# Attention before a mixture of experts: a shorter argmax chain, a first pair taken head by head, and batch 0's routing moved to the last pair

## The chip, the cores and the metric

The kernel runs on one core of one Trainium2 chip. The metric is the device time of one execution in microseconds (us). The engines are TensorE (PE; its weight loads, PEld, overlap its matmuls), VectorE (DVE), ScalarE (ACT), GpSimd (POOL) and SyncE (SP), which issues most DMAs. TensorE's clock has two levels, 1.2 and 2.4 GHz; a row's granted clock of 0.50 is the lower one.

## The reference

Only attention and the routing bear on the change. A query sees the keys of its own cluster; a token goes to one of eight experts.

```python
q_assign = np.argmax(np.einsum('bhsd,hcd->bhsc', q_n, c_n), axis=-1)
k_assign = np.argmax(np.einsum('bhsd,hcd->bhsc', k_n, c_n), axis=-1)
mask = q_assign[:, :, :, None] == k_assign[:, :, None, :]
scores = np.where(mask, scale * np.matmul(q, k.transpose(0, 1, 3, 2)), -1000000000.0)
attn = np.exp(scores - np.max(scores, axis=-1, keepdims=True))
out = np.matmul(attn / (np.sum(attn, axis=-1, keepdims=True) + 1e-09), v)
logits = x @ w_gate
e_idx = np.argmax(logits, axis=1)
```

Batch 2, heads 8, sequence 768, head size 64, 16 clusters. The expert layer (8 experts, 512 to 1024 to 512) and a dense layer (512 to 2048 to 512) follow.

## The kernel before

Attention takes two heads of a batch as a pair: pairs 0 to 3 are batch 0, pairs 4 to 7 batch 1. A head has six tiles of 128 queries, so a pair is 12 steps and attention 96. `run` (L476) goes through iterations i from -1. Iteration i issues the score matmuls of step i+1 (`qk_mm`, L363: two groups of QA by KA over 128 rows, two of QB by KB over 80, which hold the masks in rows 64 to 79), the softmax of step i (`soft`, L386: a reduction on VectorE, an exponential on ScalarE), the next stage of step i-1 and, seven steps late, the product with V (`pv`, L449). The last pair is cut in two groups of tiles so that routing can begin early.

Probabilities must be transposed. A third of the steps, and all of the last pair, do it on TensorE (`onpe`, L376; `turn`, `high`, `low2`). The others convert to 16 bits (`soft` on ScalarE, or `low` on VectorE where `dve`, L382, says so), GpSimd subtracts the low part (L438), and SP transposes two steps by DMA (L442), followed by one zero fill of a routing table from `bgdma`, if any is left.

Beside this runs the preparation of the next pair, placed by step in a list (`plan`, L256) that is written out by hand: load of q and k (L169), split in high and low halves (`halves`, L323), eight transposing tasks (`turned`, L172, with copies of half a head by DMA, L298), scores against the centroids (`scores`, L184), the argmax chain (`best`, L195), and the masks (`masks`, L333), which ScalarE evicts and four DMAs of SP put in place. The V of a pair's heads is scaled and split on GpSimd (`split_v`, L146); the scale of a batch is found by `load_v` (L114). A task at r runs in iteration base + r; within an iteration the first half of its tasks stand ahead of `pv`, the rest behind it.

Pair 0 has nothing ahead of it: `first` (L214) splits and transposes both heads, finds both argmaxes and then makes the masks (`masks1`, L344); `setup` (L65) normalises the centroids. Up to L501 the program's order is left to a scheduler; from there on each engine keeps the written order (L580).

When a pair's output is done, `pair` (L675) transposes it and adds its share of the router's logits; after a batch's last pair `route` (L709) picks experts, ranks the tokens (matmuls into `rk`), and scatters six tiles of rows by indirect DMA on GpSimd (`scatter`, L777). `run` takes one stage of it per iteration, and two where i - base is 9. Three PSUM buffers of the tag T serve all transposes, scores and routing; two hold scores of steps, one the output.

## Time and profile before

| | us |
|---|---|
| three runs | 834.8, 837.65, 840.44 |
| median of the runs | 837.65 |
| profiled execution | 835.05 |
| its span, first to last instruction | 833.1 |

The span is what the rows below count from. The clock line is TensorE's granted clock. Shares of busy time are averages over stages with different limits. The stages, by time: lead-in to 26.84, eight pairs to 292.67, the last outputs and routing to 324.77, experts to about 550, the dense layer to the end.

### The profile page before, as it was taken

To read this page: it belongs to the slowest core of one execution; us is meant where nothing else is said; L and a number is where in the kernel's file an instruction comes from. 1 tells how busy PE (TensorE), PEld (TensorE's weight loads), DVE (VectorE), ACT (ScalarE), POOL (GpSimd) and SP (SyncE) were. 2 spreads that over 40 slices of the span, in tenths; PEclk is the share of its full clock that TensorE was granted. 3 is DMA by queue.
4 is the path that set the end of the run, shared out by engine and by line. 5 is a ranking of instruction groups with operands and counts; after the bars stand their busy time and mean duration, and the time that the engine had idled before them with its cause. 6 is when DMAs were issued, how large, how long until landed. Compare 5 with 4: busy or idle time off the path is not lost. (4 is left out here: it accounts for less than half of the span.)

```text
span 833.1 us, 14096 instructions
## 1 busy us (share of the span) xinstructions
PE 760.7 (91%) x5478; PEld 642.5 (77%) x5478; DVE 486.5 (58%) x879; ACT 430.3 (52%) x695; POOL 326.4 (39%) x269
## 2 busy tenths in 40 slices
PE   5869889998899868999999999889999999999996
PEld 5658878987788755888897887667678788878885
DVE  5777797787758757466654677489932322231222
ACT  3666877867747534465555666477822322221221
POOL 1578677777775025645343455145510000000000
PEclk9979999889979977999999999999999999999999
DMA  5199999896696326688664874555500100010001
GB/s 155 23 213 245 206 205 197 174 180 148 159 165 103 123 103 225 219 291 271 221 217 150 299 233 142 190 212 173 181 1 1 51 0 1 1 50 1 1 0 54
DMA packets 132648, 116.31 MB, mean 140 GB/s; under 512 B 97719, under 2 KB 103863, under 8 KB 132576
## 3 DMA queue, kind: packets, MB, share of 16 engines
q1 hardware_dynamic: 128624, 106.27, 47.7%
q0 software_dynamic: 3952, 9.08, 3.8%
q8 instruction: 44, 0.72, 0.3%
q14 instruction: 28, 0.23, 0.1%
HBM read 71.67 MB, written 18.45 MB: 108 GB/s over the span
## 5 line engine op out<-in xcount | busy, mean ns | idle before, releaser
L859 POOL TENSOR_TENSOR w<-stage,w 128x512 fp32r<-128x512 f32 (+1 forms) x54 | 102.5, 1903 | 120.5 <-ACT w L854 109.5
L1190 PE MATMUL hp<-XH,w 128*128 128x512 f32 (+1 forms) x392 | 125.4, 397 | 2.5 <-DVE sg L1197 2.1
L854 ACT ACTIVATE w<-stage 128x1024 fp32r<-128x1024 f32 (+1 forms) x104 | 96.3, 940 | 51.4 <-DMA stage<-in_moe_w 25.2
L394 ACT ACTIVATE p<-sp,m 128x768 f32<-128x768 f32 x96 | 86.7, 903 | 54.0 <-DVE m L392 53.7
L1169 PE MATMUL op<-w,GH 128*128 128x512 f32 x384 | 112.2, 394 | 0.0
L392 DVE TENSOR_REDUCE m<-sp 128x1 f32<-128x768 f32 x96 | 91.4, 952 | 28.9 <-PE sp L373 28.4
L438 POOL TENSOR_TENSOR p<-p,p 128x768 f16<-128x768 f32 x58 | 95.3, 1650 | 30.6 <-DVE p L437 23.5
L1197 DVE TENSOR_TENSOR sg<-hp,sg 128x512 f32<-128x512 f32 (+1 forms) x49 | 33.3, 679 | 117.5 <-ACT sg L1196 117.4
L955 PEld LDWEIGHTS hp<-X,w 128*128 128x128 f32 x672 | 86.7, 191 | 9.8 <-DVE HL L958 5.5
L955 PE MATMUL hp<-X,w 128*128 128x256 f32 x672 | 90.8, 285 | 3.0 <-DVE HL L958 2.1
L1190 PEld LDWEIGHTS hp<-XH,w 128*128 128x128 f32 x392 | 74.0, 190 | 21.4 <-DVE sg L1197 3.5
L1196 ACT ACTIVATE sg<-hp 128x512 f32<-128x512 f32 (+1 forms) x49 | 28.9, 589 | 116.7 <-PE hp L1190 115.6
L859 DVE TENSOR_TENSOR w<-stage,w 128x1024 fp32r<-128x1024 f32 x50 | 69.0, 1386 | 31.3 <-ACT w L854 29.9
L1169 PEld LDWEIGHTS op<-w,GH 128*128 128x128 f32 x384 | 71.9, 188 | 17.1 <-ACT GH L854 0.4
L462 PE MATMUL o<-vh,pt 128*128 128x66 f16 x576 | 67.3, 202 | 11.7 <-DVE xb L471 6.7
L1190 PE MATMUL hp<-XL,w 128*128 128x512 f32 (+1 forms) x196 | 75.7, 394 | 1.9 <-DVE XL L859 1.9
L462 PEld LDWEIGHTS <-pt 128*128 128x128 f16 x576 | 55.7, 101 | 19.3 <-issue 11.9
L1169 PE MATMUL op<-w,GL 128*128 128x512 f32 x192 | 68.3, 397 | 1.7 <-DVE GL L859 1.7
L371 PE MATMUL sp<-KA,QA 128*128 128x384 f32 x192 | 64.9, 421 | 4.7 <-ACT p L394 4.4
L463 PE MATMUL o<-vl,pt 128*128 128x64 f16 x576 | 66.8, 198 | 0.0
L464 PE MATMUL o<-vh,pt 128*128 128x66 f16 x576 | 66.6, 199 | 0.2 <-DVE pt L429 0.2
L972 PE MATMUL yp<-w,HH 128*128 128x512 f32 x224 | 64.0, 400 | 1.5 <-ACT HH L957 1.5
(210 smaller groups left out, 1477.1 us busy)
## 6 DMA issues: line engine op xcount, KB each, us to landing
stage<-in_moe_w SPq DMA_DIRECT2D x72, 512.0 KB, 4.7
stage<-in_moe_w_in SPq DMA_DIRECT2D x16, 512.0 KB, 4.2
stage<-in_moe_w_out SPq DMA_DIRECT2D x16, 512.0 KB, 3.9
xst<-z SPq DMA_DIRECT2D x16, 258.0 KB, 3.3
xt<-xst SPq DMA_DIRECT2D x7, 516.0 KB, 4.2
vt<-in_v SPq DMA_DIRECT2D x4, 768.0 KB, 7.6
xt<-x SPq DMA_DIRECT2D x6, 512.0 KB, 4.7
out_x<-os SPq DMA_DIRECT2D x12, 256.0 KB, 2.3
```

What stands on the lines that cost most here:

```text
L371: nc.tensor.matmul(sp[:, g, :384], lhsT=QA[:, t], rhs=KAf[:, g * 384:(g + 1) * 384], start=True, stop=False)
L392: st['min'] = nc.vector.tensor_reduce(m, sv, axis=AX.XY, op=ALU.min).ins
L394: st['exp'] = nc.scalar.activation(p32, sv, AF.Exp, bias=m, scale=-1.0).ins
L438: s.nc.gpsimd.tensor_sub(p16[:, 1], p32, p16[:, 0])
L462: nc.tensor.matmul(o[:, t, 0:D + 2], lhsT=pt[:, 0, kt], rhs=vh[:, kt], start=kt == 0, stop=False)
L463: nc.tensor.matmul(o[:, t, 0:D], lhsT=pt[:, 0, kt], rhs=vl[:, kt], start=False, stop=False)
L464: nc.tensor.matmul(o[:, t, 0:D + 2], lhsT=pt[:, 1, kt], rhs=vh[:, kt], start=False, stop=kt == NT - 1)
L854: s.nc.scalar.activation(hi, src, AF.Copy)
L859: (eng or s.nc.vector).tensor_sub(lo, src, hi)
L955: nc.tensor.matmul(hp, lhsT=W1[k][w][:, f * 128:(f + 1) * 128], rhs=x[:, k, :N], start=n == 0, stop=n == 11)
L1169: nc.tensor.matmul(op[i], lhsT=g[:, i * 128:(i + 1) * 128], rhs=w, start=f == 0 and m == 0, stop=f == 15 and m == 2)
L1190: nc.tensor.matmul(h, lhsT=I[k, f // 8][w][:, fs], rhs=x[:, k, c], start=n == 0, stop=n == 11)
```

## The change

The argmax chain becomes six operations on one PSUM tile, with the high and low score side by side, and both masks come from one comparison; the query mask is turned round where it is evicted, by a factor and a bias. `first` takes head 0 to its masks before head 1's scores; head 1's subtractions and copies go to GpSimd, and its chain into the first steps. The written order holds from the first load. 12 matmuls on a constant run ahead of all. `plan` is made once, with absolute steps; a half (x.5) stands behind `pv`. V's diagonal products go to ScalarE; VectorE converts steps 8 and 9 of 12 instead of 4, 5 and 8. Zero fills begin with step 12. `high` stands ahead of the deferred evictions, and `low2` at the end of the tasks. Batch 0's `route` is kept back and taken up at iteration 86. Stages of the router per iteration follow two lists.

```diff
+    def warm(s, n):
+
+        o = s.ps_o.tile([128, NT, D + 2], F32, tag='o', name='warm')
+        for _ in range(n):
+            s.nc.tensor.matmul(o[:, 0:5].rearrange('p t d -> p (t d)')[:, 0:256], lhsT=s.ones, rhs=s.ones.unsqueeze(1).to_broadcast([128, 2, 128]), start=True, stop=True)
+
     def setup(s):
...
+                yield
         nc.vector.tensor_tensor(r, r, ss, op=ALU.mult)
...
+        nc.vector.tensor_sub(qv[:, :, 1], kv[:, :, 0], tv)
+        yield
 
     def consts(s):
...
-        nc.vector.tensor_scalar(s.mcol, mi, BIG / 16, 1.0, op0=ALU.mult, op1=ALU.max)
+        nc.vector.tensor_scalar(s.mcol, mi, (BIG + 1) / 16, -1.0, op0=ALU.mult, op1=ALU.add)
+        s.mbias = c.tile([64, 1], F32, name='mbias')
+        nc.vector.tensor_scalar(s.mbias, mi, -1.0 / 16, 1.0, op0=ALU.mult, op1=ALU.add)
...
-        nc.vector.tensor_scalar(dg[:, 1], s.ident[0:8, 0:8], g, None, op0=ALU.mult)
+        nc.scalar.activation(dg[:, 1], s.ident[0:8, 0:8], AF.Copy, scale=g)
...
-        nc.vector.tensor_scalar(dg[:, 0], s.ident[0:8, 0:8], rg, None, op0=ALU.mult)
+        nc.scalar.activation(dg[:, 0], s.ident[0:8, 0:8], AF.Copy, scale=rg)
...
-    def scores(s, hd):
+    def scores(s, hd, sides=(0, 1), clb=None):
...
-        s.clb = clb = s.T('cl')
-        cl = clb[:, :2 * NT * 2 * C].rearrange('p (a t w c) -> p a t w c', a=2, t=NT, w=2)
-        for a, (A, c1) in enumerate(((QA, s.cQ), (KA, s.cK))):
+        if clb is None:
+            clb = s.T('cl')
+        cl = clb[:, :2 * NT * 2 * C].rearrange('p (a t x) -> p a t x', a=2, t=NT)
+        for a in sides:
+            A, c1 = ((QA, s.cQ), (KA, s.cK))[a]
...
     def best(s, clb, oh, j):
 
...
-        for a in (1, 0):
-            nc.vector.tensor_reduce(s0[:, a], cl[:, a].rearrange('p t w c -> p t c w'), axis=AX.X, op=ALU.add)
-        yield
-        nc.vector.tensor_reduce(mx, s0, axis=AX.X, op=ALU.max)
-        nc.vector.tensor_tensor(s1, s0, mx.unsqueeze(3).to_broadcast([128, 2, NT, C]), op=ALU.is_ge)
-        yield
-        nc.vector.tensor_tensor(s1, s1, s.rev.unsqueeze(1).unsqueeze(1).to_broadcast([128, 2, NT, C]), op=ALU.mult)
-        nc.vector.tensor_reduce(mx, s1, axis=AX.X, op=ALU.max)
-        nc.vector.tensor_tensor(oh[:, :, j, 0], s1[:, 0], mx[:, 0].unsqueeze(2).to_broadcast([128, NT, C]), op=ALU.not_equal)
-        nc.vector.tensor_tensor(oh[:, :, j, 1], s1[:, 1], mx[:, 1].unsqueeze(2).to_broadcast([128, NT, C]), op=ALU.is_equal)
+        n = 2 * NT
+        mx = s.sm2.tile([128, n], F32, tag='mx', name='mx')
+        bc = mx.unsqueeze(2).to_broadcast([128, n, C])
+        x = clb[:, 0:n * C].rearrange('p (n c) -> p n c', c=C)
+        nc.vector.tensor_reduce(x, clb[:, 0:2 * n * C].rearrange('p (n c w) -> p n c w', w=2, c=C), axis=AX.X, op=ALU.add)
+        yield
+        nc.vector.tensor_reduce(mx, x, axis=AX.X, op=ALU.max)
+        nc.vector.tensor_tensor(x, x, bc, op=ALU.is_ge)
+        yield
+        nc.vector.tensor_tensor(x, x, s.rev.unsqueeze(1).to_broadcast([128, n, C]), op=ALU.mult)
+        nc.vector.tensor_reduce(mx, x, axis=AX.X, op=ALU.max)
+        yield
+        nc.vector.tensor_tensor(oh[:, :, j].rearrange('p t a c -> p a t c'), x.rearrange('p (a t) c -> p a t c', a=2), bc.rearrange('p (a t) c -> p a t c', a=2), op=ALU.is_equal)
         yield
 
...
+        hds = [s.heads(2 * hp + j, j) for j in range(2)]
+        lo = (nc.vector, nc.gpsimd)
+
+        def split(j):
             js = slice(j, j + 1)
             nc.scalar.activation(nq[:, js, :, 0], qt[:, js], AF.Copy)
-            nc.vector.tensor_sub(nq[:, js, :, 1], qt[:, js], nq[:, js, :, 0])
+            lo[j].tensor_sub(nq[:, js, :, 1], qt[:, js], nq[:, js, :, 0])
             nc.scalar.activation(nk[:, js, :, 1], kt[:, js], AF.Copy)
-            nc.vector.tensor_sub(nk[:, js, :, 0], kt[:, js], nk[:, js, :, 1])
-            hd = s.heads(2 * hp + j, j)
-            for n, A, w in ((nq, hd[1], -0.125), (nk, hd[3], 1.0)):
+            lo[j].tensor_sub(nk[:, js, :, 0], kt[:, js], nk[:, js, :, 1])
+
+        def turn(j):
+            for n, A, w in ((nq, hds[j][1], -0.125), (nk, hds[j][3], 1.0)):
                 for half in range(2):
                     s.turned(A, n, j, half, w)
                     s.flush()
-            nc.gpsimd.tensor_copy(hd[2][0:64], hd[1][0:64])
-            nc.vector.tensor_copy(hd[4][0:64], hd[3][64:128])
-            out.append(hd)
-            yield 'setup'
-        for j in range(2):
-            s.scores(out[j])
-            for _ in s.best(s.clb, oh, j):
-                pass
-        for j in range(2):
-            yield from s.masks1(oh, out[j], j)
-            s.ready[b, hp, j] = out[j]
-            yield 'head'
+        split(0)
+        turn(0)
+        yield
+        nc.gpsimd.tensor_copy(hds[0][4][0:64], hds[0][3][64:128])
+        split(1)
+        nc.scalar.activation(hds[0][2][0:64], hds[0][1][0:64], AF.Copy)
+        clb = s.scores(hds[0], (1, 0))
+        turn(1)
+        for _ in s.best(clb, oh, 0):
+            pass
+        nc.gpsimd.tensor_copy(hds[1][2][0:64], hds[1][1][0:64])
+        nc.gpsimd.tensor_copy(hds[1][4][0:64], hds[1][3][64:128])
+        for _ in s.masks1(oh, hds[0], 0):
+            pass
+        s.ready[b, hp, 0] = hds[0]
+        yield
+        clb = s.scores(hds[1])
+        yield
+        yield from s.best(clb, oh, 1)
+        yield from s.masks1(oh, hds[1], 1)
+        s.ready[b, hp, 1] = hds[1]
+        yield
 
     def out(s):
         if s.oev:
...
-        if pi + 2 < len(pairs):
-            add(3 if g0 else -1, lambda: s.load_qk(*pairs[pi + 2]))
...
-        if z:
-            for r in (-1, 0, 0, 1, 1):
-                add(r, nx(g0))
-            for r in (3, 3, 4, 4, 5, 6, 6, 6):
-                add(r, nx(vg))
-        for h, r in enumerate((7, 9) if z else (1, 2)):
-            add(r, sp(h))
-        if pi == 1:
-            s.v1 = s.load_v(1)
-        for r in {1: (3, 6, 10), 2: (6, 10), 3: (4, 5, 6, 6)}.get(pi, ()):
+        for r in (-0.5, 0.0, 0.5, 1, 1.5, 2, 2.0, 2.0):
+            add(r, nx(g0))
+        for r in (1.5, 1.5, 2, 3.5, 3.5, 4.5, 6, 7.0):
+            add(r, nx(vg))
+        s.v1 = s.load_v(1)
+        for r in (14.0, 17.5, 24.0, 32.0, 35.0, 40.0, 41.0, 42.0, 42.5):
             add(r, nx(s.v1))
-        if pi + 1 < len(pairs):
-            b, hp = pairs[pi + 1]
...
-            tr8 = [(j, a, half) for j in range(2) for a in range(2) for half in range(2)]
-            for (j, a, half), r in zip(tr8, (2, 2, 3, 3, 4, 4, 5, 5) if z else (-1, -1, -1, 0, 0, 0, 3, 3)):
-                add(r, lambda j=j, a=a, half=half: tr(j, a, half))
-            for j, (r, r1, r2, r3) in enumerate(((4, 5, 6, 7), (7, 8, 8, 9)) if z else ((1, 2, 3, 4), (4, 5, 6, 7))):
-                add(r, lambda j=j: sc(j))
-                for q in (r1, r2, r3):
-                    add(q, bst(j))
...
-            add(9 if z else 8, m)
-        if pi + 2 < len(pairs):
-            for i, r in enumerate((7, 8) if not z else (8, 10)):
-                add(r, lambda i=i: s.halves(pairs[pi + 2], i))
+        for p, (b, hp) in enumerate(pairs):
+            o = 12 * p
+            for h, r in enumerate((8.0, 8.5) if p == 0 else (0.0, 1.5)):
+                add(o + r, lambda b=b, h=2 * hp + h: s.split_v(b, h))
+            if p:
+                s.prepare(add, p, pairs[p], o - 12)
...
+        if not z:
+            add(1.5 if p == 2 else o - 12 + -2.0, lambda: s.load_qk(b, hp))
+        for i, r in enumerate((0.5, 1.0) if z else (6.5, 8.5) if p == 2 else [o - 12 + r for r in (6.0, 7.0)]):
+            add(r, lambda i=i: s.halves(pair, i))
...
+        tr8 = [(j, a, half) for j in range(2) for a in range(2) for half in range(2)]
+        for x, r in zip(tr8, (1.5, 1.5, 2.0, 2.5, 3.5, 3.5, 5.5, 5.5) if z else (-1.5, -0.5, 0.0, 0.5, 0.5, 0.5, 3.5, 3.5)):
+            add(o + r, lambda x=x: tr(*x))
+        for (j, a), r in zip(((0, 0), (0, 1), (1, 0), (1, 1)), (4.0, 5.0, 7.0, 7.0) if z else (1.0, 1.0, 4.0, 4.0)):
+            add(o + r, lambda j=j, a=a: sc(j, a))
+        for i, r in enumerate((7.0, 7.0, 7.0, 7.5, 8.5, 9.5, 9.5, 9.5) if z else (2.5, 2.5, 4.5, 4.5, 5, 5.0, 6.0, 7.5)):
+            add(o + r, lambda j=i // 4: next(ch[j]))
...
+        add(o + (9.5 if z else 8.0), m)
...
-        s.defer.append(lambda: nc.scalar.activation(mk, mp[0:64, :NT * 128].rearrange('p (t n) -> p t n', t=NT), AF.Copy, scale=s.mcol))
+        s.defer.append(lambda: nc.scalar.activation(mk, mp[0:64, :NT * 128].rearrange('p (t n) -> p t n', t=NT), AF.Identity, scale=s.mcol, bias=s.mbias))
...
-                    nc.scalar.activation(dst, src, AF.Copy)
+                    nc.scalar.activation(dst, src, AF.Copy, scale=-1.0, bias=1.0)
...
-        return st['i'] % 12 in (4, 5, 8)
+        return st['i'] % 12 in (8, 9)
...
-                if s.bgdma:
+                if s.bgdma and i >= 12:
...
+        traced = nc.cur_bb.bb.instructions
+        first = len(traced)
...
+        s.load_qk(*pairs[1])
+        s.after_load()
+        vg = s.load_v(0)
+        next(vg)
...
+        st = s.setup()
         s.consts()
+        s.warm(12)
+        next(st)
         next(g0)
-        s.setup()
-        s.load_qk(*pairs[1])
-        if s.after_load:
-            s.after_load()
-        for x in g0:
-            if x == 'head':
-                break
-        vg = s.load_v(0)
-        traced = nc.cur_bb.bb.instructions
-        first = len(traced)
-        next(vg)
+        next(st)
+        next(g0)
...
-            s.flush()
             if 2 <= i < n + 2 and s.onpe(steps[i - 2]):
                 s.high(steps[i - 2])
+            s.flush()
...
-            now = []
-            while todo and todo[0][0] <= i - base:
-                now.append(todo.pop(0)[1])
-            if late:
-                now.append(lambda st=steps[i - 2]: s.low2(st))
-            for f in now[:len(now) // 2]:
-                f()
+            while todo and todo[0][0] <= i:
+                todo.pop(0)[1]()
...
-            for f in now[len(now) // 2:]:
-                f()
+            while todo and todo[0][0] < i + 1:
+                todo.pop(0)[1]()
+            if late:
+                s.low2(steps[i - 2])
             if s.late and i >= s.late[0][0]:
                 rg.append(s.router(s, *s.late.pop(0)[1:]))
-            for k in range(2 if i < n - 2 else 6):
+            if i == 86:
+                rg.append(s.route0)
+                free = True
+            for k in range((1, 1, 0, 0, 1, 1, 1, 2, 0, 2, 1, 1)[i % 12] if i < n - 12 else (1, 1, 1, 0, 1, 1, 1, 1, 0, 2, 0, 2)[i % 12] if i < n - 2 else 6):
                 if i >= n - 2:
                     s.flush()
-                if rg and (i >= n - 2 or k == 0 or (i - base) % 12 == 9 and i < n - 12) and (free or not (1 <= i < n - 12 and s.onpe(steps[i - 1]))):
+                if rg and (free or not (1 <= i < n - 12 and s.onpe(steps[i - 1]))):
...
-        if hp == 3:
+        if hp == 3 and b == 0:
+            att.route0 = s.route(b, att, g)
+        elif hp == 3:
...
-        yield
+        yield 'free'
+        nc.vector.tensor_tensor(e2, rk[:, :, 0:E], oh, op=ALU.mult)
...
-        nc.vector.tensor_tensor(e2, rk[:, :, 0:E], oh, op=ALU.mult)
```

## Rows read from the trace of the kernel before

**Rows 1.** The page, part 2: granted TensorE clock in 40 slices, tenths of full speed.

```profile
PEclk9979999889979977999999999999999999999999
```

**Rows 2.** Windows cut at each pair's first reduction: stretch, length, busy (instructions), clock, DMA share, GB/s.

```profile
0.00:26.84 26.84, 16.57 (x73) 13.65 (x74) 14.66 (x59) 8.42 (x16) 3.79 (x20) 1.00 0.39 120
26.84:63.35 36.51, 27.62 (x161) 23.40 (x161) 27.21 (x47) 25.61 (x37) 26.63 (x22) 0.86 0.63 136
63.35:96.47 33.12, 29.79 (x399) 27.41 (x397) 25.65 (x49) 23.20 (x38) 24.49 (x22) 0.95 1.02 230
96.47:126.26 29.79, 27.59 (x363) 24.97 (x361) 25.46 (x48) 23.21 (x38) 23.07 (x21) 1.00 1.02 202
126.26:158.82 32.56, 30.55 (x366) 28.13 (x364) 25.79 (x54) 23.68 (x39) 23.51 (x21) 0.90 0.94 185
158.82:192.05 33.23, 31.63 (x391) 29.24 (x388) 26.50 (x51) 25.52 (x43) 24.84 (x21) 0.90 0.95 177
192.05:225.44 33.39, 26.28 (x322) 22.93 (x321) 25.32 (x62) 22.28 (x37) 24.28 (x23) 0.95 0.74 162
225.44:263.63 38.19, 35.91 (x387) 32.69 (x385) 23.62 (x47) 22.63 (x38) 23.82 (x23) 0.82 0.70 130
263.63:292.67 29.04, 25.73 (x386) 24.00 (x383) 21.46 (x39) 18.78 (x33) 8.22 (x10) 1.00 0.60 141
292.67:324.77 32.10, 21.39 (x199) 14.51 (x197) 22.22 (x83) 12.11 (x21) 9.26 (x10) 0.73 0.36 124
```

**Rows 3.** Windows again, of attention's stretches at the lower level, and the sum of all six.

```profile
47.95:58.19 10.24, 9.29 (x40) 8.12 (x39) 8.96 (x21) 6.44 (x10) 6.35 (x7) 0.50 1.18 241
...
239.10:252.75 13.65, 13.65 (x107) 12.73 (x104) 5.85 (x13) 2.24 (x3) 7.31 (x5) 0.50 0.67 127
...
sum 44.36, PE 42.29 PEld 38.94 DVE 29.50 ACT 19.89 POOL 22.74; mean PE 7.05 PEld 6.49 DVE 4.92 ACT 3.31 POOL 3.79
```

**Rows 4.** Timeline of the lead-in: start, length, engine, line, operation, tiles, [idle before, releaser].

```profile
4.88 0.56 DVE L227 TENSOR_TENSOR nk<-kld,nk 128x384 fp32r<-128x384 f32 x1
...
6.55 0.52 ACT L224 ACTIVATE nq<-qld 128x384 fp32r<-128x384 f32 x1 [1.70 <-DMA qld<-in_q]
...
12.18 1.49 PE L178 MATMUL tp<-ident,nq 128*128 128x128 f32 x6
...
14.60 1.44 PE L193 MATMUL cl<-cQ,QA 128*128 128x32 f32 x6
...
22.21 0.81 PE L353 MATMUL mp<-identb,oh 128*16 128x128 bf16 x6 [2.33 <-DVE oh L210]
...
24.18 0.56 DVE L360 TENSOR_SCALAR KB<-mp 16x384 fp32r<-16x384 f32 x1 [0.18 <-PE mp L353]
...
26.84 0.96 DVE L392 TENSOR_REDUCE m<-sp 128x1 f32<-128x768 f32 x1
...
26.95 0.84 PE L373 MATMUL sp<-KB,QB 80*128 80x384 f32 x2
```

**Rows 5.** Timeline of TensorE in pair 0, two of its waits.

```profile
46.63 0.39 PE L139 MATMUL vps<-vdg,one 8*128 8x16 f32 x2 [3.10 <-DVE vdg L136]
...
62.66 0.59 PE L373 MATMUL sp<-KB,QB 80*128 80x384 f32 x2 [2.33 <-DMA QB<-mk]
```

**Rows 6.** TensorE's waits of 26 to 297 us (total, times, longest); then GpSimd's timeline.

```profile
PE o L462 <- DMA pt<-p: 5.0, 3, 1.8
...
215.22 1.11 POOL L779 DMA_INDIRECT xst<-xb,slot  x1 [0.18 <-PE ptp L418]
...
228.85 1.00 POOL L779 DMA_INDIRECT xst<-xb,slot  x1 [0.17 <-issue]
```

**Rows 7.** Lines by form, 26 to 297 us: count, then busy, mean ns of one.

```profile
L203 DVE TENSOR_REDUCE cl<-cl 128x96 f32<-128x192 f32 x28 | 10.2, 364 | 7.5 <-PE cl L193 7.0
...
L743 DVE TENSOR_TENSOR r_d<-lacc,moe_oh 128x48 f32<-128x48 f32 x1 | 0.2, 200 | 0.0
```

**Rows 8.** The conversion on VectorE by its line: minimum, median and maximum ns.

```profile
L437 DVE CAST p<-p x21: 549/552/2541, 39.8 to 257.0; 128x768 f16<-128x768 f32 x21
```

More of the change, by code (lines that the diff above doesn't have):

```diff
@@ L77, in setup @@
         nc.vector.tensor_scalar(r.bitcast(I32), r.bitcast(I32), -1.0, float(1597463007), op0=ALU.mult, op1=ALU.add)
-        for _ in range(3):
+        for i in range(3):
             nc.vector.tensor_tensor(r2, r, r, op=ALU.mult)
@@ L90, in setup @@
         s.cQ = c.tile([128, 16 * C], F32R, name='cQ')
-        kv = s.cK.rearrange('p (h w c) -> p h w c', h=8, w=2)
+        kv, qv = (x.rearrange('p (h c w) -> p h w c', h=8, w=2) for x in (s.cK, s.cQ))
         tv = tp[:, :128].rearrange('p (h c) -> p h c', h=8)
@@ L254, in flush, with plan @@
                 d.pop(0)()
-    def plan(s, pi, pairs, g0=None, vg=None):
+    def plan(s, pairs, g0, vg):
         nc = s.nc
@@ L1223, in build @@
             att = Att(tc, c3, q, k, v, centroids, const, ident, xb, router=m.pair)
+            att.ones = m.ones
             m.att = att
```

76 lines of the change are left out of this document (34 added, 42 removed).

## The prediction, made before the result was known

> **What bounds the kernel now.** I began with the page's clock line: TensorE's clock is full nearly everywhere, and the slices well under it lie in the first two fifths [rows 1]. Next came the table of stretches, cut where the first reduction of each of the eight pairs starts [rows 2]. Every edit lies in the first 325 us of the 833: the lead-in (26.84 us), pairs 0 to 7, and the passage to the experts (32.10 us). What follows is paced by its own matmuls and moves as a block, so a microsecond saved before 325 is one of the total.
>
> Read the pairs against each other. Pair 2 ran all of its 29.79 us at granted clock 1.00 with TensorE busy 27.59: that is what a pair costs undisturbed. Pairs 1, 3, 4, 5 and 6 do nearly the same work in 33.12, 32.56, 33.23, 33.39 and 38.19, that is 3.33, 2.77, 3.44, 3.60 and 8.40 more, 21.5 us in all [rows 2]. Their clock is 0.82 to 0.95. The six stretches of attention at the lower level (granted 0.50: 1.2 of 2.4 GHz) add up to 44.36 us, the longest 13.65, in pair 6 [rows 3]. TensorE had stood still shortly before the long ones: three times for the transposed probabilities, 5.0 us together [rows 6], and in pair 0 for the scale of V, 3.10 us [rows 5]. So a short wait is paid twice, as idle time and then as a slow stretch. Pair 0 (36.51) and pair 7 (29.04, other work) are read by themselves.
>
> **The change part by part.** All sums are against the profiled execution, 835.05 us with a span of 833.1; the median of the three runs, 837.65, lies 2.6 above it.
>
> *Lead-in.* Before, the first reduction starts at 26.84. ScalarE, in the order the scheduler gave it, splits head 1 before it evicts head 0's transposes and so waits 1.70 for head 1's load; both heads' scores and argmax chains then stand before head 0's masks [rows 4]. After, head 0 goes through alone. I follow its path with the same rows. Its last split ended at 5.44; eight small centroid operations now stand ahead of it on VectorE, so 5.7. Then 12 transposes at 1.49 for six and one eviction (0.52, as the split of the same size): 9.2. Twelve score matmuls, two sixes at 1.44 that overlap a little, 2.7: 11.9; the centroids are ready before, hidden by the transposes. Head 1's 12 transposes follow on TensorE, 3.0, to 14.9, and cover the argmax chain (2.4, below), which ends at 14.3. Masks: from the first matmul at 22.21 to the end of the second copy at 24.74 is 2.5: 17.4. Of the four matmuls of the first step two wait for that copy, 0.84: the first reduction starts at about 18.4. Gain **8.4**. The table's 1.00 for this stretch misleads: the two score matmuls that take 0.84 here take 0.59 in pair 0 [rows 4, 5], so these rows are at the lower level. Bounds: if the 12 new warming matmuls raise the clock, the TensorE terms halve and it starts near 15.8 (gain 11); if in the hand-written order a load or a GpSimd copy stands in the way, as the 1.70 did and once more beside it, 21.3 (gain 5.5). The warming itself I cost at nothing: it needs only a constant, and no transpose can start before the load has landed and been split; without that cover, 12 matmuls of 256 columns take no longer than the 12 transposes, 3 us.
>
> *Pair 0.* It loses a stall: the V scale, where VectorE's chain, a matmul and a copy stood in one step, is spread over steps 4.5, 6 and 7, its two diagonal products go to ScalarE, and the first zero fills wait for step 12. That is 3.10, and at most half of the slow stretch of 10.24 behind it, 5.1 [rows 3, 5]. It gains head 1's scores and chain, 2.7 on TensorE and 2.4 on VectorE, which lie beside other work, since TensorE is busy 27.62 and VectorE 27.21 of 36.51 [rows 2]. The wait of 2.33 for a mask at its end [rows 5] stays, as masks move from step 9 to 9.5. Between 8 us gained and 2.5 lost (all of the chain on the path) I take **3.0**, nearest the stall alone.
>
> *The argmax chain.* Eight VectorE operations a head become six: two reductions to 96 columns (0.364 each [rows 7]) become one, for which I take 0.57 (bounds 0.364 and 0.73), and two comparisons become one; with five at about 0.36 that is 2.4. About 0.3 a head is saved, 4.8 us over 16 heads, none of it alone on the path. The chain is cut in four places instead of three and ends half a step later. The mask's eviction takes a bias besides its factor, on ScalarE, which is busy 23.21 of 29.79 in pair 2 [rows 2]: nothing.
>
> *Pairs 1, 3, 4.* The V splits on GpSimd go one step earlier, to 0 and 1.5. The next loads go one step earlier too, off the place just ahead of the DMA transpose that was late. The conversions of steps 4 and 5 go to ScalarE, and that of 9 comes to VectorE. Behind the splits on GpSimd waits the subtraction of step 2, behind that the DMA transpose on SP, behind that TensorE. The conversion takes 0.55 undisturbed and up to 2.54 [rows 8]. The Trainium skill (SBUF — State Buffer, Who interferes with whom) says that a VectorE copy in a two-port mode and a GpSimd operation lock each other out for a whole instruction; the spread of 0.55 to 2.54 agrees, and by that rule the conversion added at step 9 can meet the lock too, which at 0.7 in each of seven pairs would give back about 5 us and make the time 820. From the rows alone: the excess of the three pairs is 9.5 [rows 2]; none of it gained is one bound, all of it the other; I take half, **4.8**.
>
> *Batch 0's routing.* It leaves pairs 5 and 6. Six scatters from 215.22 to 229.85, about 1.0 each and some tenths before the next [rows 6], stand among GpSimd's subtractions; the last transposes of pair 5 landed late, and the 13.65 of slow clock followed. With them go two dozen VectorE operations of 0.2 [rows 7]. The excess of the two pairs is 12.0; I take three quarters of pair 6's and half of pair 5's, 6.3 + 1.8 = **8.1** (bounds 4 and 12). The work comes to pair 7, where GpSimd is busy 8.22 and VectorE 21.46 of 29.04 [rows 2]: 7.6 us of room for 4.8 of work, but in a stage that goes step by step through reduction, exponential, transpose and copy. It is also put ahead of pair 6's router, which so falls into the last two steps: six transposes, 12 narrow matmuls and an eviction, at full clock half of the lead-in's 1.49 and 2.7 and 0.5, up to 3 us on the tail of 32.10. Cost 0 to 6, taken **2.0**.
>
> Sum: 8.4 + 3.0 + 4.8 + 8.1 - 2.0 = 22.3. 835.05 - 22.3 = 812.75; with the 2.6 by which the median lies higher, **815**. With every bound good the gain is 40, with every bound bad 1; the likeliest case by itself spans 806 to 824.
>
> **Rivals.** *The middle pairs keep their stalls.* The waits for DMA move to another transfer, since the number of transfers in pairs 1 to 4 hardly changes: then only the lead-in (8.4) and 6 of the routing are won, 2.0 are lost: 12.4, so about 825. For it: the three late transposes were late by under 2 us each, and another wait of that size may be followed by a slow stretch too. Against it: pair 2, with the same transfers, has no slow stretch.
>
> *Slower: the masks come late.* The chain ends at 7.5 and the masks follow at 8.0, where a full step lay between. Behind the mask's eviction wait four DMAs on SP, and behind them the next pair's scores on TensorE. Pair 0 shows that wait, 2.33 [rows 5]. If all seven boundaries wait so long, each followed by half of a mean slow stretch (44.36 / 6 / 2 = 3.7 [rows 3]): 7 x 6.0 = 42, which makes 857. It decides from 22.3 / 7 = 3.2 us a boundary. Against it: three steps lie between the masks and their use in every pair but the first, and the zero fills no longer stand before the first.
>
> *No change that can be told.* The lead-in wins only 5.5 and pair 0 loses 2.5, since its first steps now carry head 1; the routing gives 4 and the tail takes 6 of it: about 1 us, 833 to 838 with a little of the pairs' 4.8.
>
> **How the numbers follow.** The forecast has 0.57, kept stalls 0.21, no change 0.12, late masks 0.10. One per cent, about what a measurement of this kernel can tell, is 8.4 us, so faster is under 829.3: all of the forecast and nearly all of the kept stalls, 0.77; within one per cent 0.13; slower 0.10. The low end, 800, leaves out a twentieth, with both the lead-in and the pairs near their good bounds; the high end, 834, takes in the kept stalls and the better part of no change. Predicted: 815, 800 to 834.
>
> **What would show it.** The first reduction at 16 to 21 us and no wait for the V scale; pairs 1 to 6 each under 32 us with few stretches at the lower level, and pair 6 near pair 2; no scatter before pair 7 and six in it, GpSimd idle around them; the time from pair 7's start to the first expert matmul (61.1 us before, the last two stretches of [rows 2]) no more than 6 longer. The forecast is wrong if the first reduction is later than 21, if a wait for a mask stands at most boundaries, or if pair 6 keeps a slow stretch of 10 us or more without any scatter.

## The result, and the profile after

The changed kernel took 805.09 us (median of four runs, 803.4 to 807.06) where the kernel before took 836.22 beside it: ratio 0.9615, 95% interval 0.9582 to 0.9649. Its profiled execution has a span of 805.3 us. It was measured twice more, in two later groups of runs on two chips, each time beside the kernel before: ratio 0.975 (0.967 to 0.983; 819.8 us against 839.7) and 0.9678 (0.9644 to 0.9712; 809.4 us against 836.5). Ratios and medians here leave out runs over 1.5% above the fastest of their kernel (in the second measurement three of the changed kernel's six, whose median over all six is 825.39), and two profiles, the changed kernel's second and that of the kernel with the scatters kept, are of such runs. The gain is 31, 20 and 27 us.

The changed kernel's table of stretches, cut as in [rows 2] except that the last one runs from pair 7's start to the first expert matmul (61.14 us before: the last two stretches of [rows 2]). Columns: stretch, length, busy of TensorE, its weight loads, VectorE, ScalarE and GpSimd (instructions), clock, DMA share, GB/s.

```profile
0.00:18.03 18.03, 14.02 (x68) 11.17 (x68) 9.52 (x46) 8.77 (x16) 6.58 (x23) 1.00 0.71 222
18.03:54.57 36.54, 28.95 (x185) 24.82 (x185) 26.36 (x47) 26.81 (x42) 28.49 (x23) 0.77 0.50 96
54.57:85.83 31.26, 29.05 (x403) 27.38 (x399) 23.33 (x43) 24.68 (x40) 22.93 (x20) 0.95 1.05 223
85.83:115.44 29.61, 26.94 (x366) 24.70 (x363) 24.57 (x44) 25.19 (x40) 23.50 (x21) 1.00 1.05 205
115.44:144.11 28.67, 28.59 (x370) 26.43 (x367) 22.87 (x47) 24.40 (x41) 22.91 (x20) 0.94 1.03 211
144.11:174.25 30.14, 27.93 (x367) 25.99 (x364) 22.26 (x42) 24.49 (x40) 23.25 (x21) 0.94 1.11 203
174.25:205.04 30.79, 27.80 (x366) 25.95 (x363) 22.19 (x41) 24.52 (x40) 23.18 (x21) 0.94 1.00 187
205.04:231.39 26.35, 26.20 (x364) 24.50 (x361) 22.03 (x42) 22.90 (x37) 19.28 (x19) 1.00 0.82 157
231.39:295.64 64.25, 48.34 (x596) 40.05 (x592) 47.12 (x144) 30.61 (x55) 22.68 (x27) 0.85 0.53 155
```

Against [rows 2]: the lead-in lost 8.8 us, pair 0 nothing, pairs 1, 3 and 4 together 8.8, pair 2 0.2, pairs 5 and 6 together 14.4; pair 7 with what follows grew by 3.1. That is 29.1 by the first expert matmul, of which the experts gave back 1.3. Pair 6 went from the longest pair to the shortest. Its DMA share is the lowest among pairs 1 to 6: no q and k and no zero fill is left to move there.

TensorE's waits in attention, from the view of waits (16 to 290 us; total, times, longest), three rows of it: the wait for V's scale of [rows 5] is gone, one for GpSimd's split of pair 1's q is new, and those for the transposed probabilities, 5.0 us before [rows 6], are still there, with 6.5.

```profile
PE o L487 <- DMA pt<-p: 6.5, 4, 3.0
...
PE tp L190 <- POOL nq L356: 2.6, 1, 2.6
...
PE sp L398 <- DMA KB<-mk: 1.3, 1, 1.3
```

### The profile page after: what moved, and what is told of

It reads as the page before. It is cut to its first block, busy times and chain, and to the rows that moved or that the text cites. A ratio compares the mean times of both kernels' runs of the same rounds, so it can differ in the third digit from the quotient of the medians.

```text
span 805.3 us, 14091 instructions
## 1 busy us (share of the span) xinstructions
PE 742.3 (92%) x5490; PEld 630.4 (78%) x5490; DVE 468.2 (58%) x834; ACT 437.0 (54%) x707; POOL 326.9 (41%) x272
## 4 chain that ended last, share of the span: by engine, by line
PE 54%; DMA 15%; DVE 10%; POOL 7%; ACT 6%; issue 6%; SPq 0%; POOLq 0%; DVEq 0%; ACTq 0%
PE op L1192 13%; PE hp L1213 13%; DMA stage<-in_moe_w 6%; DMA pt<-p 4%; PE yp L995 4%; PE hp L978 4%; PE sp L396 3%; PE sp L398 3%; POOL w L882 3%; PE ptp L443 2%; ACT w L877 2%; PE tp L190 2%; PE o L487 2%; PE o L489 2%; DVE w L882 1%
## 5 line engine op out<-in xcount | busy, mean ns | idle before, releaser
L877 ACT ACTIVATE w<-stage 128x1024 fp32r<-128x1024 f32 (+1 forms) x104 | 96.3, 940 | 50.7 <-DMA stage<-in_moe_w 25.1
L417 DVE TENSOR_REDUCE m<-sp 128x1 f32<-128x768 f32 x96 | 91.5, 953 | 33.9 <-PE sp L398 30.0
L1220 DVE TENSOR_TENSOR sg<-hp,sg 128x512 f32<-128x512 f32 (+1 forms) x49 | 33.3, 679 | 117.5 <-ACT sg L1219 117.5
L487 PE MATMUL o<-vh,pt 128*128 128x66 f16 x576 | 66.2, 200 | 8.8 <-DMA pt<-p 6.5
L487 PEld LDWEIGHTS <-pt 128*128 128x128 f16 x576 | 54.6, 100 | 17.6 <-issue 8.7
L489 PE MATMUL o<-vh,pt 128*128 128x66 f16 x576 | 65.0, 197 | 0.7 <-DVE pt L454 0.6
L396 PE MATMUL sp<-KA,QA 128*128 128x384 f32 x192 | 60.9, 400 | 3.6 <-ACT p L419 3.2
```

Of the source, the lines that this page charges most:

```text
L396: nc.tensor.matmul(sp[:, g, :384], lhsT=QA[:, t], rhs=KAf[:, g * 384:(g + 1) * 384], start=True, stop=False)
L417: st['min'] = nc.vector.tensor_reduce(m, sv, axis=AX.XY, op=ALU.min).ins
L487: nc.tensor.matmul(o[:, t, 0:D + 2], lhsT=pt[:, 0, kt], rhs=vh[:, kt], start=kt == 0, stop=False)
L489: nc.tensor.matmul(o[:, t, 0:D + 2], lhsT=pt[:, 1, kt], rhs=vh[:, kt], start=False, stop=kt == NT - 1)
L877: s.nc.scalar.activation(hi, src, AF.Copy)
```

## The experiments

The kernels ran in three groups, each group on one chip, so totals are compared within a group or as ratios to the kernel before. Stage lengths come from one profile of each kernel, from the same table of stretches (the changed kernel has three); the last column is pair 7 to the first expert matmul.

| us | lead-in | pair 0 | 1 | 2 | 3 | 4 | 5 | 6 | 7 and on |
|---|---|---|---|---|---|---|---|---|---|
| before | 26.84 | 36.51 | 33.12 | 29.79 | 32.56 | 33.23 | 33.39 | 38.19 | 61.14 |
| changed, first | 18.03 | 36.54 | 31.26 | 29.61 | 28.67 | 30.14 | 30.79 | 26.35 | 64.25 |
| changed, second | 17.56 | 34.99 | 32.06 | 34.93 | 33.62 | 27.14 | 31.16 | 26.35 | 71.69 |
| changed, third | 18.51 | 35.45 | 39.14 | 28.43 | 27.75 | 30.06 | 31.40 | 26.32 | 62.88 |
| routing back | 16.82 | 34.99 | 31.81 | 32.57 | 33.74 | 32.68 | 31.87 | 31.58 | 60.90 |
| scatters kept | 17.22 | 34.95 | 32.89 | 29.44 | 30.75 | 33.91 | 30.86 | 26.33 | 65.57 |
| loads at step 2 | 16.19 | 34.95 | 31.49 | 30.64 | 28.66 | 28.99 | 28.56 | 26.33 | 63.09 |
| loads and fills | 16.83 | 39.60 | 37.18 | 26.68 | 27.09 | 26.62 | 26.67 | 26.71 | 62.65 |

### Batch 0's routing put back, and its scatters alone kept

```diff
-        if hp == 3 and b == 0:
-            att.route0 = s.route(b, att, g)
-        elif hp == 3:
+        if hp == 3:
...
-            if i == 86:
-                rg.append(s.route0)
-                free = True
-            for k in range((1, 1, 0, 0, 1, 1, 1, 2, 0, 2, 1, 1)[i % 12] if i < n - 12 else (1, 1, 1, 0, 1, 1, 1, 1, 0, 2, 0, 2)[i % 12] if i < n - 2 else 6):
+            for k in range((2 if i % 12 == 9 and i < n - 12 else 1) if i < n - 2 else 6):
```

> The changed kernel with one part undone: batch 0's routing runs where it ran before, behind pair 3's router, one stage an iteration. Changed kernel: 805.1, pairs 5 and 6 together 57.1 us, from pair 7's start to the first expert matmul 64.2. Theory A (the routing inside pairs 5 and 6 is what made them long): the two pairs grow by 12 to 14.4, to 69 to 71.6, six scatters stand in them, a long wait for the transposed probabilities comes back with a slow stretch behind it; the tail gives back 3; total 814 to 817. Theory B (the other placement of V splits, loads and conversions, which also holds in these pairs, brought a part, 3 us a pair as in pairs 1, 3 and 4): the two pairs grow by 6 to 8.5; total 808 to 811. Theory C (pair 6's long slow stretch was no matter of the routing): the two pairs stay within 2 us of 57.1; total 802 to 804.

The second kernel has the same pace of the router, but hands only the six scatters to iteration 86:

```diff
-        for t in g:
-            yield 'free'
-            s.scatter(s.xst, s.slot[:, b * NT + t:b * NT + t + 1], xb[:, t], E * CAP)
+        sc = s.send(b, g)
+        if b == 0:
+            att.route0 = sc
+        else:
+            yield from sc
```

> As the kernel with the routing back in pairs 4 to 6, but its six scatters alone are kept for the last pair; the VectorE operations and the rank matmuls of batch 0's routing stay in pairs 4 to 6. If the scatters on GpSimd are what delays the subtractions, and these the DMA transposes: pairs 5 and 6 together 57 to 59.5 as in the changed kernel, total 803 to 807. If the two dozen small VectorE operations and the rank matmuls do it: the pairs stay as long as with the whole routing back (if that is 69 to 71.6, then over 66), total 812 to 817. If the scatters cost their time in the last pair: pair 7 and what follows to the first expert matmul 2 to 4 us above those of the kernel with the routing back.

Measured: 816.5 us, ratio 0.973 (0.9646 to 0.9814), with the routing back; 801.9 (two runs), 0.9571 (0.9481 to 0.9662), with the scatters kept. The totals' intervals overlap a little, so the reading rests on the pairs, in one profile of each kernel. Windows of pairs 5 and 6 with the routing back, and rows of GpSimd, SP and TensorE at the end of pair 5:

```profile
182.61:214.48 31.87, 25.98 (x337) 22.81 (x336) 24.21 (x57) 24.68 (x40) 27.14 (x26) 0.97 0.96 201
214.48:246.06 31.58, 31.45 (x376) 29.65 (x374) 22.41 (x43) 22.52 (x36) 21.61 (x20) 0.87 0.73 140
```

```profile
200.84 1.01 POOL L797 DMA_INDIRECT xst<-xb,slot  x1 [0.17 <-issue]
201.88 1.67 POOL L463 TENSOR_TENSOR p<-p,p 128x768 f16<-128x768 f32 x1
203.57 4.33 SPq L467 DMA_TRANSPOSE pt<-p  x1
208.63 0.68 SPq L367 DMA_DIRECT2D QB<-mk  x1
213.47 0.98 PE L398 MATMUL sp<-KB,QB 80*128 80x384 f32 x2 [3.40 <-DMA KB<-mk]
```

and with the scatters alone kept for the last pair:

```profile
179.16:210.02 30.86, 29.31 (x351) 26.68 (x350) 24.41 (x58) 24.23 (x40) 23.20 (x21) 0.89 0.88 165
210.02:236.35 26.33, 26.18 (x363) 24.48 (x360) 22.03 (x41) 22.87 (x37) 19.25 (x19) 1.00 0.81 157
```

With the routing back the two pairs take 63.5 us, without the scatters 57.2, as in the changed kernel (57.1). The rows show a way for the 6.3 us, though not the one that theory A named: neither pair has a wait for transposed probabilities. A subtraction stands behind a scatter on GpSimd, a transpose behind the subtraction on SP, and the masks behind the transpose; TensorE waits 3.40 us for a mask, and a stretch of 10.2 us at the lower level follows, in pair 6. With the scatters kept no such wait stands there. The 5.3 us of pair 6 are outside what it took in the twelve profiles without scatters in it (26.3 to 27.8); the 1.0 of pair 5, which took 26.7 to 32.7 in them, is not. So the scatters are worth about 6 us in these pairs, not 14.4: theory B's size, with the scatters as the cause.

The VectorE operations and rank matmuls of the routing, which both kernels have in pairs 4 to 6, cost nothing that shows in pairs 5 and 6. Pair 4, where the first of them stand, took 32.7 and 33.9, against 27.1 to 30.1 in the changed kernel, each with a wait of about 3 us for transposed probabilities; a cost there is not excluded. In the last pair and behind it the scatters cost 4.7 in these two profiles (65.57 against 60.90), where 2 to 4 were expected; the changed kernel's first and third profile, with 64.25 and 62.88, would make it 2.0 to 3.4. The total with the routing back came to theory A's because pairs 2 to 4 were long too (99.0), where no scatter is; pairs 2 and 3 come before all of batch 0's routing and have the same instructions in both kernels, and took 66.3 and 60.2.

### Splits and loads back; conversions back

```diff
-            for h, r in enumerate((8.0, 8.5) if p == 0 else (0.0, 1.5)):
+            for h, r in enumerate((8.0, 8.5) if p == 0 else (1.0, 2.0)):
...
-            add(1.5 if p == 2 else o - 12 + -2.0, lambda: s.load_qk(b, hp))
+            add(1.5 if p == 2 else o - 12 + -1.0, lambda: s.load_qk(b, hp))
```

> The changed kernel with the V splits on GpSimd back at steps 1 and 2 of a pair and the loads of q and k back one step later. Changed kernel: pairs 1, 3 and 4 together 90.1 us, total 805.1. Theory (the splits and loads stood ahead of the subtraction that a DMA transpose waits for): the three pairs grow by 6 to 9, waits for the transposed probabilities of over 1 us in each, pair 5 grows by 1 to 3; total 812 to 817. Rival (the conversions that went from steps 4 and 5 of VectorE to ScalarE brought it): the three pairs within 2 us of 90.1; total 804 to 807.

```diff
-        return st['i'] % 12 in (8, 9)
+        return st['i'] % 12 in (4, 5, 8)
```

> The changed kernel with the conversions of steps 4, 5 and 8 of each twelve on VectorE, as before, instead of 8 and 9. If these conversions brought the gain of pairs 1, 3 and 4 (8.9 us together): the three pairs grow by 6 to 9, the conversion takes up to 2.5 us at some places, total 812 to 817. If the splits and loads brought it: the three pairs within 2 us of 90.1, total 804 to 807. If both brought a half, as I summed them: 3 to 5 us in the three pairs, total 808 to 811.

Measured: 814.88, ratio 0.9722 (0.9666 to 0.9777), and 816.68, 0.976 (0.9678 to 0.9842). Pairs 1, 3 and 4 took 96.3 and 95.2 us. Beside the first profile of the changed kernel (90.1) that is 6.2 and 5.1 more, as if each carried it; beside its third (97.0) it is less. The group had no run of the changed kernel, and the intervals of that one's ratios (0.9582 to 0.983 in all) take these two in. What each edit brings by itself stays open.

### The changed kernel again

> The changed kernel itself once more, to see what of a stage's length is its own and what is chance: the kernel with the scatters kept and the one with the whole routing back run the same instructions in pairs 2 and 3, and took 60.2 and 66.3 us for them. If stage lengths are the kernel's own: each pair within 1 us of the first profile (36.5, 31.3, 29.6, 28.7, 30.1, 30.8, 26.3), total 803 to 807. If the clock's changes and the DMA's landings fall differently from one execution to the next: single pairs differ by 2 to 5 us from the first profile, the lead-in lies between 16 and 18, and their sum by less, total 800 to 812.

Measured: 819.8 us. Pair 6 is the same to the hundredth, pairs 1 to 4 are not: together they took 119.7, 127.8 and, in the third profile, 125.4 (before: 128.7). Windows of pairs 2 and 3 in the second profile:

```profile
84.61:119.54 34.93, 31.73 (x366) 29.75 (x364) 25.18 (x44) 24.52 (x39) 22.95 (x20) 0.82 1.02 176
119.54:153.16 33.62, 30.32 (x370) 28.11 (x367) 23.26 (x47) 25.27 (x42) 23.14 (x21) 0.85 0.99 185
```

The same pairs took 29.61 and 28.67 in the first. Each holds one wait, of 3.2 and 3.3 us, for transposed probabilities and a slow stretch behind it. The gain that I would have read from the first profile for pairs 1, 3 and 4 (8.8) is 6.1 in the second and 2.0 in the third; pair 2 gave 0.2, lost 5.1 and gave 1.4. On this chip pair 7 and what follows took 69.6 to 71.8 us in all four kernels of the group, on the other chips 61 to 66, and the rest of the program 512 to 523, where the others took 506 to 515. There is no profile of the kernel before from it, so where the smaller gain of this chip was lost stays open.

### Pair 0, the argmax chain, the warming

Three small edits, in the group of the changed kernel's second measurement (819.8 us). Pair 1's split earlier:

```diff
-        for i, r in enumerate((0.5, 1.0) if z else (6.5, 8.5) if p == 2 else [o - 12 + r for r in (6.0, 7.0)]):
+        for i, r in enumerate((-0.5, -0.5) if z else (6.5, 8.5) if p == 2 else [o - 12 + r for r in (6.0, 7.0)]):
```

> The changed kernel with the high halves and subtractions of pair 1's q and k at step -0.5 instead of 0.5 and 1. In the changed kernel TensorE waits 2.58 us at 20.95 for GpSimd's subtraction of pair 1's q, and pair 0 takes 36.5 us, where 33.5 were forecast. Theory (that wait took the place of the V scale's, and so pair 0 won nothing): the wait is gone, pair 0 at 33 to 34.5, total 2 to 4 us less than the changed kernel run beside it. Rival (pair 0 is paced by ScalarE and GpSimd, busy 26.8 and 28.5 of 36.5, and by the lower clock that its many short waits bring): the wait is gone, pair 0 within 1 us of 36.5, total within 1.5.

Measured: 823.3 (ratio 0.9812, 0.9739 to 0.9885), not told apart from the changed kernel. The subtraction now starts at 16.31 in GpSimd's earlier idle time and TensorE does not wait for it, but pair 0 took 34.8 us where the changed kernel beside it took 35.0. So that wait was not what kept pair 0 long, as the rival said. Its reason, that ScalarE and GpSimd pace the pair, is not shown by it.

The chain with eight operations again:

```diff
-        nc.vector.tensor_reduce(x, clb[:, 0:2 * n * C].rearrange('p (n c w) -> p n c w', w=2, c=C), axis=AX.X, op=ALU.add)
+        for a in range(2):
+            nc.vector.tensor_reduce(x[:, a * NT:(a + 1) * NT], clb[:, 2 * a * NT * C:2 * (a + 1) * NT * C].rearrange('p (n c w) -> p n c w', w=2, c=C), axis=AX.X, op=ALU.add)
...
-        nc.vector.tensor_tensor(oh[:, :, j].rearrange('p t a c -> p a t c'), x.rearrange('p (a t) c -> p a t c', a=2), bc.rearrange('p (a t) c -> p a t c', a=2), op=ALU.is_equal)
+        for a in range(2):
+            nc.vector.tensor_tensor(oh[:, :, j, a], x[:, a * NT:(a + 1) * NT], bc[:, a * NT:(a + 1) * NT], op=ALU.is_equal)
```

> The changed kernel with eight VectorE operations a head again in the argmax chain, in the same places and on the same layout: the first reduction cut in two of 96 columns, the last comparison in two. My working: 0.15 us for the reduction and 0.25 to 0.3 for the comparison a head, about 0.4 to 0.5, 7 us of VectorE time over 16 heads, nearly none of it on the path; head 0's chain alone lies on the lead-in: total 0 to 2 us more than the changed kernel run beside it, the lead-in 0.4 longer. Rival (VectorE's queue feeds the reductions, and the masks of the next pair come later): 4 to 8 us more, with waits for a mask at the boundaries.

Measured: 825.6 (0.9811, 0.9753 to 0.9869) beside 819.8; the intervals of the ratios overlap, so the totals do not decide between the two forecasts. The profiles speak against a cost: the lead-in took 17.4 beside 17.6, and the first expert matmul, behind all the chains, came at 305.3, where the other three kernels of the group had 305.7 to 310.8.

Without the 12 matmuls ahead of all:

```diff
-        s.warm(12)
```

> The changed kernel without the 12 matmuls on a constant ahead of all. If they cost nothing and give nothing (forecast): first reduction at 17 to 18.4, total within 1.5 us of the changed kernel run beside it. If they raise the clock for the transposes of the lead-in in part of the executions (full clock stood from 4.2 to 11.1 us in three of the five profiles with them): no full clock before 11 us without them, first reduction at 18 to 19, total 1 to 2 us more.

Measured: 822.18 (0.9783, 0.9724 to 0.9841): not told apart from the changed kernel. By the length of its matmuls the clock is at the lower level to about 28 us, and the first reduction starts at 18.50. Of the twelve profiles with the warming, five show the full level before 11 us from the first transposes on (six of them in 0.85 us instead of 1.51) and a first reduction at 16.2 to 16.8; the others show none or a shorter one there, and 17.2 to 18.5. So the warming may give 1 to 2 us in some executions, and no cost of it shows; one profile without it does not prove more.

### What makes the transposes late

SP issues the DMA transposes, the zero fills, the loads and the masks in one queue. SP's timeline of the changed kernel, pair 4 into 5 (start, length, line, operation, tiles):

```profile
169.58 0.56 SPq L367 DMA_DIRECT2D QB<-mk  x1
...
172.10 0.57 SPq L181 DMA_DIRECT2D qld<-in_q  x1
172.72 0.50 SPq L181 DMA_DIRECT2D kld<-in_k  x1
173.32 6.11 SPq L467 DMA_TRANSPOSE pt<-p  x1
179.48 0.58 SPq L1249 DMA_DIRECT2D xst<-z  x1
180.17 0.58 SPq L324 DMA_DIRECT2D KB<-KA  x1
180.86 5.54 SPq L467 DMA_TRANSPOSE pt<-p  x1
```

and of pair 6, where nothing is loaded or filled:

```profile
203.40 3.62 SPq L467 DMA_TRANSPOSE pt<-p  x1
208.42 0.50 SPq L324 DMA_DIRECT2D KB<-KA  x1
209.05 4.41 SPq L467 DMA_TRANSPOSE pt<-p  x1
```

From 142 to 199 us each row of SP starts within 0.2 us of the end of the one before it: the queue has no gap. Issuing a transpose holds it for 3.6 us at best and 6.1 with 768 KB of loads of q and k just ahead; the next stands behind. The transpose of 180.86 is the one that TensorE waited 2.99 us for; it landed at 191.2. In the kernel before it was no different, one step later:

```profile
162.80 0.77 SPq L169 DMA_DIRECT2D qld<-in_q  x1
163.61 0.78 SPq L169 DMA_DIRECT2D kld<-in_k  x1
164.49 0.51 SPq L298 DMA_DIRECT2D KB<-KA  x1
165.10 6.64 SPq L442 DMA_TRANSPOSE pt<-p  x1
```

Four kernels test this, the changed one a third time among them, on one chip:

> The changed kernel a third time, beside the three below on the same chip. Pair 6 at 26.3 to 26.4 again, since it was 26.34 and 26.35 in its two profiles; pairs 1 to 4 together 119 to 129 (119.7 and 127.7 so far), with two or three waits of 2 to 4 us for transposed probabilities; total 803 to 827, as on the two chips before.

```diff
-                if s.bgdma and i >= 12:
-                    s.bgdma.pop(0)()
+                for _ in range(3 if i < 12 else 0 if i < 72 else 1):
+                    if s.bgdma:
+                        s.bgdma.pop(0)()
```

> The changed kernel with its 18 zero fills issued behind the DMA transposes of pair 0, three each, and the last three in pair 6; none in pairs 1 to 5. In the changed kernel SP's queue stands without a gap in pairs 1 to 5: a transpose takes it 3.6 us in pair 6, where nothing is loaded and filled, and 4 to 7 in the others. Theory (SP's queue and the transfers beside it make the transposes late in pairs 1 to 5, fills among them): each of these pairs loses 1 to 2.5 us against the third look at the changed kernel, waits for transposed probabilities fall under 1.5, pair 0 gains up to 2; total 5 to 10 us less. Rival (the loads ahead of a transpose do it, the fills behind it do not): pairs 1 to 5 as before them, total within 3.

```diff
-            add(1.5 if p == 2 else o - 12 + -2.0, lambda: s.load_qk(b, hp))
+            add(1.5 if p == 2 else o - 12 + 2.0, lambda: s.load_qk(b, hp))
```

> The changed kernel with the loads of q and k for the pair after next four steps later, at step 2 of a pair instead of step 10 of the one before: between the second and the third transpose, where four steps lie, and not right ahead of the first of two that follow within two steps. Theory (the load of 768 KB ahead of a transpose stretches it from 3.6 to 6 us, and the next one stands behind it): waits for transposed probabilities in pairs 2 to 5 fall under 1.5 us, each of the pairs loses 1 to 3, total 4 to 10 us less than the third look. Rival (the load only shifts to the next transposes): waits of the same size at other steps, total within 3. Against both: the halves wait for the load, over 3 more.

> Both edits together, the zero fills in pair 0 and 6 and the loads at step 2. If fills and loads each take part in making the transposes late: no wait of over 1 us for one in pairs 1 to 5, these pairs at 27 to 28.5 each, close to pair 6's 26.3, total 10 to 16 us less than the third look at the changed kernel. If the waits come from GpSimd's subtractions and not from SP's queue: total within 3.

Measured: changed kernel 809.43 (804.59 to 811.13), fills in pair 0 805.78 (0.9659, 0.9618 to 0.97), loads at step 2 **798.43** (797.25 to 800.92; ratio 0.9569, 0.9539 to 0.9598), both 804.48 (0.9631, 0.9592 to 0.9669). Moving the loads alone is worth 11.0 us and beats both kernels; every one of its six runs is below every one of the changed kernel's. The fills alone are worth 3.7, where 5 to 10 were expected and the intervals overlap; both edits 5.0, where 10 to 16 were expected.

Where the loads' 11.0 us lie is only in part where the theory put them. In pairs 2 to 5 TensorE's waits for transposed probabilities are 0.3 us in all, where the changed kernel beside it has 4.7 (view of waits, 93 to 211 us there and 82 to 200 here):

```profile
PE sp L398 <- DMA KB<-mk: 4.2, 3, 2.2
...
PE o L487 <- DMA pt<-p: 0.3, 1, 0.3
```

But the waits for masks there rose from 1.3 to 4.2, and the four pairs took 116.9 us against 117.6: in them the wait only changed its place, and the 1 to 3 us a pair that were expected did not come. Of the 11.0 us between the two profiles at the first expert matmul, pair 1 has 7.6 and the lead-in, where the two kernels are the same, 2.3. The changed kernel has the loads for pair 3 at step 10 of pair 0, ahead of two transposes; behind these stands the load of batch 1's V, whose maximum VectorE takes ahead of softmax reductions. Its third profile, with TensorE's wait (view of waits, 50 to 96 us):

```profile
54.05 6.06 SPq L467 DMA_TRANSPOSE pt<-p  x1
60.84 6.90 SPq L467 DMA_TRANSPOSE pt<-p  x1
67.79 2.96 SPq L130 DMA_DIRECT2D vt<-in_v  x2
77.22 0.95 DVE L135 TENSOR_REDUCE vam<-vt 128x2 f32<-128x768 f32 x1 [5.97 <-DMA vt<-in_v]
```

```profile
PE o L487 <- DMA pt<-p: 4.5, 2, 2.6
```

and with the loads at step 2, where TensorE has no such wait in pair 1 and VectorE does not wait for V:

```profile
51.03 3.60 SPq L467 DMA_TRANSPOSE pt<-p  x1
56.20 4.81 SPq L467 DMA_TRANSPOSE pt<-p  x1
61.06 1.31 SPq L130 DMA_DIRECT2D vt<-in_v  x2
```

So the transposes were shorter without the loads ahead of them, and in these two profiles that paid in pair 1, through the transposed probabilities and through V. But in the changed kernel's first two profiles pair 1 took 31.3 and 32.1, with a wait for V of 1.15 and none; how much of the 11.0 comes this way in other executions is not shown.

With the fills gone too, pairs 2 to 5 hold no wait of TensorE at all that the view lists, and run at full clock:

```profile
93.61:120.29 26.68, 26.54 (x366) 24.75 (x363) 24.50 (x44) 24.29 (x39) 22.64 (x21) 1.00 0.96 182
120.29:147.38 27.09, 27.00 (x370) 24.95 (x367) 22.77 (x47) 25.15 (x43) 23.61 (x21) 1.00 0.99 187
147.38:174.00 26.62, 26.49 (x367) 24.72 (x364) 22.08 (x42) 24.36 (x40) 23.12 (x21) 1.00 0.96 186
174.00:200.67 26.67, 26.54 (x366) 24.76 (x363) 22.09 (x41) 24.38 (x40) 23.15 (x21) 1.00 0.99 187
```

They take 107.1 us together, against 117.6 in the changed kernel beside it. The rival that the fills do nothing falls with pairs 2, 4 and 5 of the kernel with the fills moved alone (27.1, 26.6 and 26.7; its pair 3, with one wait of 4.0, took 34.7): of the 48 such pairs in the twelve profiles that have the fills there, the shortest took 27.14. So what SP has to issue makes these pairs long. Whether by the queue's own time or by what the fills and loads take of the DMA engines (share 0.96 to 0.99 here, up to 1.11 in the changed kernel) is not told apart. But the fills, three at a time, make pairs 0 and 1 pay, so both edits together win less than the loads alone. The first row is TensorE's, pair 0's end, the second VectorE's, pair 1:

```profile
55.41 0.98 PE L398 MATMUL sp<-KB,QB 80*128 80x384 f32 x2 [5.72 <-DMA QB<-mk]
```

```profile
77.41 0.95 DVE L135 TENSOR_REDUCE vam<-vt 128x2 f32<-128x768 f32 x1 [4.49 <-DMA vt<-in_v]
```

The masks stand behind the fills on SP, and so does the load of batch 1's V.

## Why the prediction was right or wrong

Predicted 815 (800 to 834), measured 805.1 and, in the later groups, 809.4 and 819.8. The sign and the size hold; the terms did not all come as written. Of the signs named, the first reduction, the V scale and pair 6 came in all three profiles; that pairs 1 to 6 each stay under 32 us came in the first alone (up to 34.9 and 39.1 in the others).

**Lead-in, 8.4.** Right in mechanism and size: 8.8, 9.3 and 8.3. The first reduction of the argmax takes 0.566 us, where 0.57 was taken, and no price of the warming shows. Two slips did no harm: the terms add up to 18.2, not 18.4, and with the TensorE terms halved they give about 14, not 15.8. The earliest first reduction of all, with the full level up to about 11 us, was at 16.2.

**Pair 0, 3.0.** Wrong: 0.0, 1.5 and 1.1. The V scale's wait went, and the new wait for GpSimd's split (2.6) took its place in two of the three profiles. But taking that away as well won nothing. The step that failed is the inference from a removed stall, with half of the slow stretch behind it, to a shorter pair. Nor does the clock decide: before, the rows from 26.84 to about 37.5 us are at the lower level too, by the length of their matmuls, so pair 0 had about 21 us of it and not 10.24, and after it had 17.1, 13.7 and, counted the same way, 16 in the three profiles, without getting shorter by more than about 1.5. The longer slow stretch of the first profile, 40.79 to 54.45, followed no wait of TensorE over 0.9 us within 9 us. What would shorten pair 0 was not found.

**The argmax chain, nothing alone on the path.** No profile speaks against it; the totals could not tell 2 us from 6.

**Pairs 1, 3, 4, 4.8.** Near on the average (8.8, 6.1, 2.0; mean 5.6, or 4.4 with pair 2), but that is luck as far as these profiles go, against one profile of before, and the reason I gave is half wrong. I wrote that the loads leave the place just ahead of the late transpose. They leave it for the place ahead of the transpose before that one, behind the masks; the waits for transposed probabilities stayed, 6.5, 9.8 and 9.2 us in the three profiles of attention. So the rival that the middle pairs keep their stalls described these pairs better than the forecast, and my argument against it, that pair 2 has the same transfers and no slow stretch, was chance: pair 2 had 12.3 us of it in the second profile, and took 34.4 and 33.3 us in the kernels with the split earlier and without the warming, which leave it as it is. The rule of the Trainium skill (SBUF — State Buffer, Who interferes with whom) that I priced at 5 us cost nothing like it: VectorE's 14 conversions took 0.55 at the median and 0.98 at most, where before they took up to 2.54 [rows 8].

**Batch 0's routing, 8.1.** Right in that the scatters delay what stands behind them, though in the one profile with them back it was a mask that came late; and too small: 14.4, 14.1 and 13.9 for the two pairs. The mis-sized term is the base. I took pair 2 (29.79 us) as what a pair costs undisturbed; pair 6 without scatters takes 26.3 to 26.7 in eleven of twelve profiles, and pairs 2 to 5 take 26.6 to 27.1 with loads and fills out of the way. The scatters by themselves are about 6.3 of the 14.4; the other 8.1, from 71.6 before to the 63.5 of the kernel with the routing back, came with the rest of the change or was the chance of that one profile of before.

**The tail, 2.0 lost.** Right: 3.1 and 1.7 in the first and third profile; in the second, 71.69 against 61.14 on another chip, it can't be told. The last wait grew. TensorE waits 4.59 us for the scattered rows, 3.12 before, and the second of the last two scatters takes 1.97 us, 0.97 before, while VectorE subtracts expert weights beside it:

```profile
292.34 1.97 PE L935 MATMUL etp<-ident,xt 128*128 128x128 f32 x8 [4.59 <-DMA xt<-xst]
```

```profile
282.28 1.76 POOL L802 DMA_INDIRECT xst<-xb,slot  x1 [4.30 <-DVE o_cnt L824]
284.35 1.97 POOL L802 DMA_INDIRECT xst<-xb,slot  x1 [0.30 <-issue]
```

**The sum.** 22.3 was forecast, 29.1 came by the first expert matmul in the first profile: pair 0 gave 3.0 less, pairs 5 and 6 gave 6.3 more, pairs 1, 3 and 4 gave 4.0 more in that execution, and the tail took 1.1 more. The rival that the masks come late fell: one or two waits of 1.2 to 1.7 us for a mask in each of the three profiles, where seven of 2.33 were priced.

## What to carry to other kernels

Give the queue that issues DMAs a busy time like an engine's, and list what stands ahead of each transfer that something waits for: the loads of q and k, moved by four steps, were worth 11 us in the total, more than most of this change's parts. Then look where the time went: here it came, as far as two profiles show it, in another pair than the theory named, and in part through another transfer. Before a stage serves as the undisturbed measure, look for one with less traffic that is shorter still. A stage length from one profile is one draw; here a pair's length moved by up to 8 us between profiles of one kernel, and only what repeats to the hundredth (pair 6) or separates all the runs (the loads' total) is a reading.
